# A pad of 1,344 bytes that gives all operands of two feed-forward layers one SBUF offset

## The chip, the cores and the metric

The kernel runs on one core of a Trainium2 chip. The metric is the device time of one execution in microseconds (us); the profile's span runs from the first to the last instruction of that execution.

## The reference, cut to what matters

Attention over 4 x 8 heads of 576 positions (a window of 32, half of the heads dilated by 4) gives 2,304 tokens of 512 features. Two feed-forward layers follow, 512 to 2,048 to 512, all in float32:

```python
x = attention(q, k, v)                       # (2304, 512)
h = x @ w_in                                 # 512 -> 2048
g = np.maximum(h, 0.0) + alpha * np.minimum(h, 0.0)
x = g @ w_out                                # 2048 -> 512
h = x @ w2_in
g = np.where(h >= 1, h, np.where(h <= -1, 0.0, (h + 1) ** 2 / 4))
return g @ w2_out
```

## The kernel before, in words

**The feed-forward work.** Each layer `ph` (0 or 1) goes through five tiles of tokens: four of 512 and one of 256 (the fourth in the first layer, the last in the second). A tile is written (ph, t) here. Within a tile, `f` runs over the 16 blocks of 128 hidden features. A pair (tile, f) is a slot; there are 160.

For each slot there are two groups of twelve matmuls: four blocks `c` of 128 features, by three products. `f_h` (lines 334 to 336, the **h group**) makes the block of h in one PSUM bank. `f_y` (lines 374 to 376, the **y group**) adds the block's part of the output to four PSUM banks. Float32 accuracy comes from three products: every operand is split into a rounded part (`xh`, `wih`, `gh`, `woh`) and the rest (`xl`, `wil`, `gl`, `wol`), and high x high, high x low and low x high are summed. Each matmul streams 512 (or 256) columns of x or g and has 128 x 128 weights of its own, loaded anew.

In iteration k the loop issues `f_h` of slot k, then `f_y` of slot k - 2. So h and y groups alternate, and h of block f is followed by y of block f - 2 (h(0) by y(14) of the tile before, h(1) by its y(15)). At the very end, y(13), y(14) and y(15) follow each other. In front of each y group and behind it, `attention_point` may put in a stage of attention: scores, transposed weights, values or output. There are 24 attention groups; six run before the loop, and the rest are spread over the first layer's first tiles.

Beside TensorE, ScalarE and VectorE make g from h (`f_g`, `f_cut`), ScalarE and GpSimd split the next block of output weights (`wo_split`, lines 320 and 321), and VectorE unpacks weights in the tiles that prepare a layer.

**Where the operands lie.** The SBUF pools are opened in the order const, wp, cv_p, xs_p, s_p, st_p (lines 75 to 80) and lie in memory in that order. Later, behind them, come sp, for the first attention groups, and then in its place wl_p, ws_p and g_p (lines 507, 509, 510). What the feed-forward matmuls read:

- `wih`, `wil`: for f < 8 in wp, for f >= 8 in wl_p
- `xh`, `xl`: in xs_p, four buffers each
- `woh`, `wol`: in ws_p, two buffers each (those of the last slot alone in cv_p)
- `gh`, `gl`: in g_p, two buffers each

All these tiles are 128 x 512 of 4 bytes, 2,048 bytes per partition, and all other tiles of wp, cv_p, xs_p, wl_p, ws_p and g_p are 2,048 or 4,096 bytes. So within a pool every tile starts at the same offset modulo 2 KB. Between xs_p and the late pools lie s_p (three tiles of 1,536 bytes) and st_p (two tiles of 24 bytes with three buffers each, in slots of 32 bytes).

Of the kernel before, what the change touches and what calls it, by code (L numbers as in the profile page):

```python
# [10 lines left out]
F32 = mybir.dt.float32  # L11
# [11 lines left out]
P = 128  # L23
# [24 lines left out]
)  # L48
TW = 512
WARM = 10  # L50
DS = D + 1

EARLY = (5, 6)
# [18 lines left out]
def attention_then_two_ffns(ctx: ExitStack, tc: tile.TileContext, a0, aqk, av, w1i, w1o, w2i, w2o, alpha, masks, ident, out):  # L72
# [8 lines left out]
    ps_h = ctx.enter_context(tc.tile_pool(name="ps_h", bufs=2, space=bass.MemoryType.PSUM))  # L81
    ps_a = ctx.enter_context(tc.tile_pool(name="ps_a", bufs=1, space=bass.MemoryType.PSUM))

    X = [const.tile([P, NT], F32, name=f"X{c}") for c in range(NC)]
    al = const.tile([P, NF], F32, name="al")
    mask = const.tile([P, NSB, KEYS], BF16, name="mask")
# [3 lines left out]
    qk = [const.tile([P, QK + KW], F32, name=f"qk{i}") for i in range(2)]  # L90
    vz = [const.tile([P, GS, 2, 4, DS], F32, name=f"vz{i}") for i in range(2)]

# [21 lines left out]
    def a_scores(i, pool, tag, add_on_pe):  # L114
# [20 lines left out]
        mx = st_p.tile([P, 2 * GS], F32, tag="mx", name="mx")  # L135
        nc.vector.tensor_reduce(mx, src, AX.X, ALU.max)
        sc_t[i] = (src, s, mx)
# [30 lines left out]
    def e_exp(i):  # L168
# [4 lines left out]
        mx = mx.rearrange("p (h n) -> p h n", h=2)  # L173
        nc.vector.tensor_reduce(mx, src, AX.X, ALU.max)
        nc.vector.tensor_tensor(
# [4 lines left out]
    def e_values(i):  # L180
# [3 lines left out]
        for n in range(GS):  # L184
            for j in range(4):
                r = slice(j * SUB, (j + 1) * SUB)
                for h in range(2):
                    p = slice(h * D, (h + 1) * D)
                    nc.tensor.matmul(ps[r, h, n * DS:(n + 1) * DS], pT[p, n, r], v[p, n, j], start=True, stop=True)  # L189
        a_norm(i, ps[:, :, :GS * DS].rearrange("p h (n d) -> p n h d", n=GS))  # L190

# [9 lines left out]
    def a_values(i, pool, tag):  # L201
        pT = pT_t.pop(i)
        ps = pool.tile([P, GS, 2, DS], F32, tag=tag, name="o_ps")
        for n in range(GS):
# [5 lines left out]
    def a_norm(i, ps):  # L210
        o = tmp(i).tile([P, GS, 2, D], F32, tag="o", name="o")
        rs = st_p.tile([P, GS, 2, 1], F32, tag="rs", name="rs")
        nc.vector.tensor_scalar(rs, ps[:, :, :, D:], 1e-9, None, ALU.add)
        nc.vector.reciprocal(rs, rs)
        nc.vector.tensor_tensor(o, ps[:, :, :, :D], rs.to_broadcast([P, GS, 2, D]), ALU.mult)
        o_t[i] = o

    def a_out(i, pool, tag):
# [8 lines left out]
        while at < len(subs):  # L227
# [4 lines left out]
            src = ps[:, at * SUB:(at + n) * SUB]  # L232
            xb = X[hp][:, b * S:(b + 1) * S]
            p0, p1 = s0 * SUB, (s0 + n) * SUB
# [66 lines left out]
    def x_split(n, c, on_pool=False):  # L301
# [3 lines left out]
        lo = xs_p.tile([P, TW], F32R, tag="xl", name="xl")  # L305
        src = X[c][:, t0:t0 + w]
        nc.scalar.activation(hi[:, :w], src, AF.Copy)
# [56 lines left out]
    def f_y(n, f):  # L364
# [12 lines left out]
        if f == NF - 1:  # L377
            for c in range(NC):
                dst = X[c][:, t0:t0 + w]
                if c % 2:  # L380
# [15 lines left out]
    with tc.manual_schedule(), ExitStack() as late:  # L396
        first = ExitStack()
        sp = first.enter_context(tc.tile_pool(name="sp", bufs=1))
        ps_e = first.enter_context(tc.tile_pool(name="ps_e", bufs=1, space=bass.MemoryType.PSUM))
        e_in = [sp.tile([P, QK + GS * 4 * DS], F32, name=f"e_in{i}") for i in range(NGB)]  # L400

# [28 lines left out]
        ps = ps_h.tile([P, TW], F32, tag="h", name="warm_ps")  # L430
        for _ in range(WARM):
            nc.tensor.matmul(ps, warm[:, :P], warm, start=True, stop=True)
# [170 lines left out]
def _attention_layout(q, k, v):  # L603
# [10 lines left out]
    ak = np.zeros((B, NGB, P, KW), q.dtype)  # L614
    av = np.ones((B, NSB, P, 4, DS), q.dtype)
    for sb in range(NSB):
# [53 lines left out]
```

## Time and profile before

| | |
|---|---|
| time, median of 3 runs | 891.58 us (890.82 to 891.71) |
| the profiled execution's own time | 891.61 us |
| its span | 889.8 us |
| TensorE busy | 871.0 us (98%), 5,470 matmuls |
| VectorE, ScalarE, GpSimd busy | 461.6, 371.6, 277.0 us |
| mean granted clock of TensorE | 0.987 |

How to read it: PE is TensorE's matmuls, PEld its weight loads, DVE VectorE, ACT ScalarE, POOL GpSimd. Matmuls are pipelined, so the durations of neighbours overlap: a row's duration is not the pace. The pace is the difference between the starts of rows that follow each other. In the timeline a line L334 that comes after a line L376 is the head of an h group, a line L374 after a line L336 the head of a y group; lines 334, 335, 336 then repeat for the four blocks c.

### The profile page before, as it was taken

To read this page: it belongs to the slowest core of one execution; us is meant where nothing else is said; L and a number is where in the kernel's file an instruction comes from. 1 tells how busy PE (TensorE), PEld (TensorE's weight loads), DVE (VectorE), ACT (ScalarE), POOL (GpSimd) and SP (SyncE) were. 2 spreads that over 40 slices of the span, in tenths; PEclk is the share of its full clock that TensorE was granted. 3 is DMA by queue.
4 is the path that set the end of the run, shared out by engine and by line. 5 is a ranking of instruction groups with operands and counts; after the bars stand their busy time and mean duration, and the time that the engine had idled before them with its cause. 6 is when DMAs were issued, how large, how long until landed. Compare 5 with 4: busy or idle time off the path is not lost.

```text
span 889.8 us, 13837 instructions
## 1 busy us (share of the span) xinstructions
PE 871.0 (98%) x5470; PEld 717.8 (81%) x5470; DVE 461.6 (52%) x769; ACT 371.6 (42%) x715; POOL 277.0 (31%) x222
## 2 busy tenths in 40 slices
PE   6889999999999999999999999999999999999998
PEld 3567778888888888998888888888888888888898
DVE  6788774433353423347776894543344334433443
ACT  3444445444354434454334343433343334333454
POOL 3355544121122122444442342222222222222243
PEclk8789999999999999999999999999999999999999
DMA  9696631131221400002442320010001000100100
GB/s 360 202 273 196 196 92 38 39 75 38 57 57 38 137 1 1 1 1 77 148 143 66 129 79 0 1 48 1 0 1 48 1 0 1 48 1 0 48 2 24
DMA packets 24832, 59.34 MB, mean 67 GB/s; under 512 B 2880, under 2 KB 10688, under 8 KB 24768
## 3 DMA queue, kind: packets, MB, share of 16 engines
q1 hardware_dynamic: 24480, 58.30, 21.0%
q8 instruction: 43, 0.70, 0.3%
q14 instruction: 21, 0.17, 0.1%
q10 hardware_dynamic: 288, 0.16, 0.1%
HBM read 53.73 MB, written 4.72 MB: 66 GB/s over the span
## 4 chain that ended last, share of the span: by engine, by line
PE 95%; DMA 2%; DVE 1%; ACT 1%; issue 1%; SPq 0%; ACTq 0%
PE h_ps L334 15%; PE y L374 15%; PE y L376 15%; PE h_ps L336 15%; PE y L375 15%; PE h_ps L335 15%; DMA e_in<-a 2%; PE s_ps L129 2%; PE o_ps L207 1%; PE x_ps L222 1%; PE t_ps L196 1%; DMA qk<-aqk 1%; PE o_ps L189 0%; PE s_ps L165 0%; ACT pT L198 0%
## 5 line engine op out<-in xcount | busy, mean ns | idle before, releaser
L321 POOL TENSOR_TENSOR wol<-wo,woh 128x512 fp32r<-128x512 f32 x160 | 207.8, 1299 | 481.6 <-ACT woh L320 481.6
L334 PE MATMUL h_ps<-xh,wil 128*128 128x512 f32 (+1 forms) x640 | 242.2, 378 | 0.4 <-DVE gl L362 0.3
L374 PE MATMUL y<-gh,wol 128*128 128x512 f32 (+1 forms) x640 | 239.3, 374 | 0.0
L336 PE MATMUL h_ps<-xh,wih 128*128 128x512 f32 (+1 forms) x640 | 237.9, 372 | 0.0
L376 PE MATMUL y<-gl,woh 128*128 128x512 f32 (+1 forms) x640 | 236.8, 370 | 0.0
L335 PE MATMUL h_ps<-xl,wih 128*128 128x512 f32 (+1 forms) x640 | 236.7, 370 | 0.0
L375 PE MATMUL y<-gh,woh 128*128 128x512 f32 (+1 forms) x640 | 236.0, 369 | 0.0
L334 PEld LDWEIGHTS h_ps<-xh,wil 128*128 128x128 f32 x640 | 121.2, 189 | 23.5 <-DVE gl L362 2.0
L336 PEld LDWEIGHTS h_ps<-xh,wih 128*128 128x128 f32 x640 | 120.9, 189 | 22.8
L374 PEld LDWEIGHTS y<-gh,wol 128*128 128x128 f32 x640 | 120.6, 188 | 21.7 <-issue 1.8
L376 PEld LDWEIGHTS y<-gl,woh 128*128 128x128 f32 x640 | 120.4, 188 | 21.8
L335 PEld LDWEIGHTS h_ps<-xl,wih 128*128 128x128 f32 x640 | 121.2, 189 | 20.7
L375 PEld LDWEIGHTS y<-gh,woh 128*128 128x128 f32 x640 | 120.6, 188 | 20.5
L353 ACT ACTIVATE g<-g,half 128x512 f32<-128x512 f32 (+1 forms) x80 | 54.5, 681 | 147.4 <-DVE g L352 147.2
L349 DVE SCALAR_TENSOR_TENSOR g<-g,al,h_ps 128x512 f32<-128x512 f32 (+1 forms) x80 | 55.3, 692 | 86.7 <-ACT g L347 86.5
L320 ACT ACTIVATE woh<-wo 128x512 fp32r<-128x512 f32 x160 | 99.2, 621 | 0.0
L356 ACT ACTIVATE gh<-g 128x512 fp32r<-128x512 f32 (+1 forms) x80 | 47.2, 589 | 120.5 <-PE y L375 80.1
L352 DVE TENSOR_SCALAR g<-h_ps 128x512 f32<-128x512 f32 (+1 forms) x80 | 50.8, 635 | 70.5 <-PE h_ps L336 70.3
L355 DVE TENSOR_TENSOR h_ps<-h_ps,g 128x512 f32<-128x512 f32 (+1 forms) x80 | 51.7, 646 | 58.9 <-ACT g L353 58.9
L362 DVE TENSOR_TENSOR gl<-h_ps,gh 128x512 fp32r<-128x512 f32 (+1 forms) x80 | 51.0, 637 | 56.6 <-ACT gh L356 56.6
L362 DVE TENSOR_TENSOR gl<-g,gh 128x512 fp32r<-128x512 f32 (+1 forms) x64 | 40.0, 626 | 70.7 <-ACT gh L356 62.8
L356 ACT ACTIVATE gh<-h_ps 128x512 fp32r<-128x512 f32 (+1 forms) x80 | 44.4, 555 | 71.4 <-PE y L375 48.2
(66 smaller groups left out, 581.2 us busy)
## 6 DMA issues: line engine op xcount, KB each, us to landing
st<-w1i SPq DMA_DIRECT2D x16, 512.0 KB, 5.0
st<-w1o SPq DMA_DIRECT2D x16, 512.0 KB, 4.5
st<-w2i SPq DMA_DIRECT2D x16, 512.0 KB, 3.4
st<-w2o SPq DMA_DIRECT2D x16, 512.0 KB, 3.3
qk<-aqk SPq DMA_DIRECT2D x36, 208.0 KB, 3.9
vz<-av SPq DMA_DIRECT2D x36, 195.0 KB, 3.9
out_t<-X SPq DMA_DIRECT2D x16, 256.0 KB, 2.0
e_in<-a SPq DMA_DIRECT2D x6, 416.0 KB, 7.4
```

The source lines that it names most:

```text
L320: nc.scalar.activation(hi, wf, AF.Copy)
L321: nc.gpsimd.tensor_tensor(lo, wf, hi.bitcast(F32), ALU.subtract)
L334: nc.tensor.matmul(ps[:, :w], wl[:, cs], xh[:, :w], start=(c == 0), stop=False)
L335: nc.tensor.matmul(ps[:, :w], wh[:, cs], xl[:, :w], start=False, stop=False)
L336: nc.tensor.matmul(ps[:, :w], wh[:, cs], xh[:, :w], start=False, stop=(c == NC - 1))
L349: nc.vector.scalar_tensor_tensor(t, t, al[:, f:f + 1], ps, ALU.mult, ALU.add)
L353: nc.scalar.activation(t, t, AF.Square, bias=half, scale=0.5)
L356: nc.scalar.activation(hi, ps, AF.Copy)
L362: (nc.gpsimd if n == order[0] else nc.vector).tensor_tensor(lo, ps, hi.bitcast(F32), ALU.subtract)
L374: nc.tensor.matmul(o, wl[:, cs], gh, start=(f == 0), stop=False)
L375: nc.tensor.matmul(o, wh[:, cs], gh, start=False, stop=False)
L376: nc.tensor.matmul(o, wh[:, cs], gl, start=False, stop=(f == NF - 1))
```

## The change

A pool of one tile of 336 float32 values (1,344 bytes per partition) that nothing reads or writes is opened after the last of the early pools and kept to the end. All that is allocated later, sp first and then wl_p, ws_p and g_p, moves up by 1,344 bytes. Nothing else is changed.

```diff
 WARM = 10
+
+PAD = 336
 DS = D + 1
...
     ps_h = ctx.enter_context(tc.tile_pool(name="ps_h", bufs=2, space=bass.MemoryType.PSUM))
     ps_a = ctx.enter_context(tc.tile_pool(name="ps_a", bufs=1, space=bass.MemoryType.PSUM))
 
+
+    ctx.enter_context(tc.tile_pool(name="pad", bufs=1)).tile([P, PAD], F32, name="pad")
     X = [const.tile([P, NT], F32, name=f"X{c}") for c in range(NC)]
```

## Rows read from the trace of the kernel before

**Rows 1.** The page: busy time by engine, and the chain that ended last.
```profile
PE 871.0 (98%) x5470; PEld 717.8 (81%) x5470; DVE 461.6 (52%) x769; ACT 371.6 (42%) x715; POOL 277.0 (31%) x222
...
PE 95%; DMA 2%; DVE 1%; ACT 1%; issue 1%; SPq 0%; ACTq 0%
```

**Rows 2.** Busy time by stretch: its ends, its length, engines, clock, DMA share, GB/s.
```profile
395.50:834.30 438.80, 438.73 (x1922) 358.80 (x1922) 237.88 (x355) 171.56 (x288) 124.27 (x96) 1.00 0.12 40
```

**Rows 3.** Groups by line and form: count | busy us, mean ns | idle before.
```profile
L334 PE MATMUL h_ps<-xh,wil 128*128 128x512 f32 x512 | 206.0, 402 | 0.1
```

**Rows 4.** Timeline of TensorE (start, duration): heads of h(0), h(8), next h(0), tile (1, 2).
```profile
657.84 0.39 PE L334 MATMUL h_ps<-xh,wil 128*128 128x512 f32 x1
...
701.79 0.40 PE L334 MATMUL h_ps<-xh,wil 128*128 128x512 f32 x1
...
746.05 0.39 PE L334 MATMUL h_ps<-xh,wil 128*128 128x512 f32 x1
```

**Rows 5.** Timeline, tile (1, 2): h(2), then y(0), its fourth matmul, then h(3).
```profile
668.83 0.39 PE L334 MATMUL h_ps<-xh,wil 128*128 128x512 f32 x1
...
671.59 0.39 PE L374 MATMUL y<-gh,wol 128*128 128x512 f32 x1
...
672.28 0.39 PE L374 MATMUL y<-gh,wol 128*128 128x512 f32 x1
...
674.32 0.39 PE L334 MATMUL h_ps<-xh,wil 128*128 128x512 f32 x1
```

**Rows 6.** The same: h(10), its fourth matmul, y(8), its fourth, then h(11).
```profile
712.86 0.40 PE L334 MATMUL h_ps<-xh,wil 128*128 128x512 f32 x1
...
713.56 0.39 PE L334 MATMUL h_ps<-xh,wil 128*128 128x512 f32 x1
...
715.62 0.40 PE L374 MATMUL y<-gh,wol 128*128 128x512 f32 x1
...
716.32 0.40 PE L374 MATMUL y<-gh,wol 128*128 128x512 f32 x1
...
718.39 0.40 PE L334 MATMUL h_ps<-xh,wil 128*128 128x512 f32 x1
```

**Rows 7.** Timeline, tile (0, 2): fourth matmul of h(3) after attention, then y(1).
```profile
267.85 0.39 PE L334 MATMUL h_ps<-xh,wil 128*128 128x512 f32 x1
...
269.89 0.39 PE L374 MATMUL y<-gh,wol 128*128 128x512 f32 x1
```

**Rows 8.** Timeline, the last tile's end: h(15), y(13), y(14) with its second, y(15).
```profile
880.29 0.28 PE L334 MATMUL h_ps<-xh,wil 128*128 128x256 f32 x1
...
881.71 0.29 PE L374 MATMUL y<-gh,wol 128*128 128x256 f32 x1
...
883.15 0.28 PE L374 MATMUL y<-gh,wol 128*128 128x256 f32 x1
883.27 0.28 PE L375 MATMUL y<-gh,woh 128*128 128x256 f32 x1
...
884.59 0.28 PE L374 MATMUL y<-gh,wol 128*128 128x256 f32 x1
```

**Rows 9.** Groups by line and form: the attention's scores.
```profile
L129 PE MATMUL s_ps<-qk 128*32 128x128 f32 x432 | 16.0, 284 | 0.7 <-DMA qk<-aqk 0.7
```

**Rows 10.** Timeline, the last tile: heads of h(4), y(2) and h(5).
```profile
848.89 0.28 PE L334 MATMUL h_ps<-xh,wil 128*128 128x256 f32 x1
...
850.32 0.28 PE L374 MATMUL y<-gh,wol 128*128 128x256 f32 x1
...
851.73 0.28 PE L334 MATMUL h_ps<-xh,wil 128*128 128x256 f32 x1
```

## The prediction

> **What bounds the kernel now.** I read the page's busy shares first. TensorE is busy 98% of the span and makes 95% of the chain that ended last; VectorE, ScalarE and GpSimd stand at 52%, 42% and 31% [rows 1]. In the stretch from 395.5 to 834.3 us, which holds the last 512-token tile of the first layer and four tiles of the second, TensorE is busy 438.73 of 438.80 us at a granted clock of 1.00, the 2.4 GHz level [rows 2]. It waits for nobody there, so the time is the number of matmuls times their pace, and nothing counts that does not change the pace.
>
> The pace is uneven. The busy means (402 ns for a 512-column matmul, [rows 3]) overlap and do not give it; starts in the timeline do. Tile (1, 2) is plain: its heads for f = 0, f = 8 and the next tile's f = 0 lie at 657.84, 701.79 and 746.05 us [rows 4]. Each half is eight iterations of an h and a y group, 192 equal matmuls, yet the halves take 43.95 and 44.26 us, 88.21 together.
>
> Inside one iteration of each half [rows 5, 6]:
> - f = 2: h takes 671.59 - 668.83 = 2.76 us, y 2.73 us; the last nine matmuls of that y take 674.32 - 672.28 = 2.04 us, 226.7 ns each.
> - f = 10: h takes 2.76 us, y 2.77 us; the last nine of y 2.07 us, the last nine of h 715.62 - 713.56 = 2.06 us, 229 ns each.
>
> **Operand offsets.** Every tile that these matmuls read is 2,048 bytes long, so its offset modulo 2 KB is that of its pool. wp and xs_p share one offset, call it A. Between them and the late pools lie s_p (3 x 1,536 bytes) and st_p (2 x 3 slots of 32), 4,800 bytes, or 704 past two times 2 KB. So wl_p, ws_p and g_p lie at B = A + 704. An h group with f < 8 reads weights and x at A; with f >= 8 it reads weights at B and x at A; a y group reads both at B (the last of all has its weights in cv_p, at A). A y group is the same in both halves: same buffers, same offsets, same PSUM banks. What differs is the h group that it follows. After one with both operands at A it takes 2.73 us, after one with weights at B 2.77 us. So a group carries the trace of the offset step in front of it.
>
> That trace dies out. In tile (0, 2) an h group at A and A comes after attention work, and its last nine matmuls run at 269.89 - 267.85 = 2.04 us, 226.7 ns each [rows 7], where h(2), just after a step from B to A, needs 2.76 us for twelve (230). The fast end of y, the fast end of this h and twelve times 226.7 (2.72 us) are my price for a group without a step. Where the offsets in a group differ (f >= 8) its end stays at 229.
>
> Nearest to a boundary without a step is the end of the kernel: y(13) and y(14) of the last tile follow each other, both at B. y(14) runs from 883.15 to 884.59 us, 1.44 us, at 0.12 a matmul from the first one on [rows 8]; nothing is disturbed at the boundary. That tile has 256 columns, so it shows the mechanism and not the price at 512.
>
> **The change, part by part.** The pad adds 1,344 bytes behind st_p, and 704 + 1,344 = 2,048: all late pools move to A. No instruction is added, nor a wait or a transfer. sp and its successors move together, so which early tile a late one overlaps, and hence what it waits for, stays. The attention's operands from X to st_p stay where they are. I cost all of that at nothing; were one of those waits longer, TensorE would show it as a gap.
>
> 1. Whole 512-column tiles without attention. 384 matmuls at 226.7 ns are 87.05 us against 88.21: 1.16 us per tile. There are five: -5.8 us.
> 2. Tiles (0, 0) to (0, 2) have 96 groups with attention matmuls between many of them: the 432 score matmuls recorded are 18 attention groups of 24 [rows 9], and three stages of each break some 54 boundaries. About 40 remain without a break. They save 1.16 us / 32 = 36 ns each: -1.4 us. At a broken boundary I take no change. Bounds: if every such group also came to 226.7, 54 x 36 ns or 1.9 us less; if each got the slower y (2.77 for 2.73), 54 x 0.04 or 2.2 us more. I take the middle, since the h of [rows 7] shows that a break can also leave the pace nearly flat.
> 3. The two 256-column tiles get worse. At one offset throughout, y(14) takes 1.44 us. Now h(15), at differing offsets, takes 881.71 - 880.29 = 1.42, h(4) 850.32 - 848.89 = 1.43 and y(2) 851.73 - 850.32 = 1.41 us [rows 8, 10]. Per tile, 8 x 0.02 + 8 x 0.01 + 8 x 0.03 = 0.48 us: +0.9 us for both.
> 4. Other engines: a faster TensorE asks for g and the split weights 1% sooner. GpSimd, the slowest per instruction, is busy 124 of 439 us in the steady stretch [rows 2]; its slack covers this. Uncovered, a lost half microsecond per iteration would eat the whole gain.
>
> Sum: -5.8 - 1.4 + 0.9 = -6.3 us. The profiled execution took 891.61 us (889.8 span and 1.8 around it), 0.03 above the median of 891.58, so it stands for the runs: 885.3 us.
>
> The Trainium skill speaks against any of this. "TensorE: Matmul & The Clock Gate", Step-by-step: what each phase is for, says that TensorE reads the streamed operand and the weights through two independent SBUF ports, and that loading the next weights takes nothing from the running matmul. By that rule offsets would not matter and the sum would be nil. Here equal y groups take 2.73 and 2.77 us by the address of weights that others used before them, which that rule does not give.
>
> **Rivals.**
> - No change. The pace comes from the alternation of groups itself (new PSUM bank, a new moving buffer, the return from column block 3 to 0), and offsets only shift its pattern: after the change some groups are quicker, some slower. For it: h groups take 2.76 us in both halves although one has equal offsets and the other not. Against it: the two kinds of y. Time 891.6.
> - Slower: all groups lock into the slow pattern. h with f < 8 already has the wanted state, both operands at A, and takes 2.76. If this is what one offset gives once a group begins afresh, each y that now takes 2.73 goes to 2.77: 8 per tile x 0.04 x 5 = 1.6 us, some 0.4 us in the earlier tiles, and the 256-column term of 0.9. Time 894.5. It decides at the first matmuls after a boundary: there h would still need over 230 ns. Against it: this h comes after a step from B to A, and the h of [rows 7], at the same offsets, settles at 226.7.
> - Half the gain. Each group keeps a short disturbance at its first three matmuls, as y in [rows 5] (0.69 us for three), because the weights' column block goes back there. All groups then take 2.73: per tile 16 x 0.03 + 8 x 0.04 = 0.8 us, five tiles 4.0, the earlier ones 1.0, less 0.9. Time 887.5.
> - More gain. The broken boundaries settle too (1.9 us), and the locked pace lies 1 ns lower than two-decimal starts tell (some 2,400 matmuls, 2.4 us). Time 881 to 883.
>
> **How the numbers follow.** Forecast 0.55, half the gain 0.16, more gain 0.09, no change 0.11, slower 0.09. About 0.2% (1.8 us) is what a measurement of this kernel can tell from no change. Faster by more than that: the first three, 0.80. Same 0.11. Slower 0.09. The forecast's own range is 883 to 888, from the bounds in 2 and 1 ns per matmul downward; the range is widened to 882.0 at the end of more gain and to 889.5 for a short disturbance with the upper bound of 2, which leaves out no change and slower, the two together 0.20.
>
> **What would show it.** In tile (1, 2) of the changed kernel both halves should take the same, near 43.5 us, and h and y alike 2.72 us. The pace should be flat across the boundary of h and y. The 256-column groups should all take 1.44 us, 0.48 us per tile more than now. TensorE should still be busy throughout. I am wrong if the halves still differ, if h(2) still takes 2.76 us, or if gaps on TensorE appear that name GpSimd or ScalarE.

## The result, and the profile after

The changed kernel takes 883.85 us (median of 5 runs, 883.60 to 885.64), the kernel before 891.71 in the same series (890.82 to 892.28). The ratio is 0.9916, 95% interval 0.9905 to 0.9927: faster by 0.84%. Forecast were 885.3 us and the range 882.0 to 889.5. The profiled execution took 883.60 us, its span is 881.8 us.

The page of the changed kernel, where [rows 1] stood before: TensorE is as large a share of the span busy as it was, and the same 5,470 matmuls keep it busy 7.6 us less.

```profile
PE 863.4 (98%) x5470; PEld 717.2 (81%) x5470; DVE 461.9 (52%) x769; ACT 371.5 (42%) x715; POOL 275.5 (31%) x222
```

Where the time went shows in the busy time by stretch, cut at the heads of the tiles. The columns are those of [rows 2]. First the kernel before (tiles (0, 0) to (0, 3); the next five, of 512 columns, in one; the last tile and the end):

```profile
31.15:145.49 114.34, 108.39 (x843) 83.85 (x841) 85.81 (x142) 50.05 (x98) 55.43 (x45) 0.96 0.56 162
145.49:247.67 102.18, 102.18 (x713) 82.97 (x709) 38.90 (x77) 46.55 (x109) 21.73 (x17) 1.00 0.24 58
247.67:347.14 99.47, 99.47 (x635) 80.70 (x634) 37.73 (x69) 41.81 (x93) 20.79 (x16) 1.00 0.16 48
347.14:395.45 48.31, 48.31 (x385) 47.32 (x384) 16.86 (x34) 23.82 (x53) 20.76 (x16) 1.00 0.00 1
395.45:834.27 438.82, 438.75 (x1923) 358.82 (x1921) 237.91 (x355) 171.60 (x288) 124.27 (x96) 1.00 0.12 40
834.27:889.80 55.53, 51.62 (x409) 50.22 (x407) 23.41 (x54) 25.70 (x54) 22.01 (x17) 1.00 0.08 29
```

The same stretches of the changed kernel:

```profile
30.48:144.19 113.71, 107.17 (x843) 82.53 (x841) 86.76 (x146) 50.38 (x99) 56.07 (x45) 0.97 0.58 165
144.19:245.56 101.37, 101.37 (x712) 82.94 (x709) 38.94 (x76) 46.48 (x109) 21.60 (x17) 1.00 0.24 58
245.56:344.15 98.59, 98.59 (x634) 80.65 (x633) 37.77 (x69) 41.88 (x93) 20.63 (x16) 1.00 0.16 48
344.15:392.82 48.67, 48.67 (x385) 47.69 (x384) 16.89 (x35) 23.87 (x53) 20.68 (x16) 1.00 0.00 1
392.82:825.97 433.15, 433.02 (x1922) 358.58 (x1921) 237.72 (x355) 171.58 (x288) 123.23 (x96) 1.00 0.12 41
825.97:881.80 55.83, 51.95 (x409) 50.56 (x407) 23.50 (x54) 25.77 (x54) 21.90 (x17) 1.00 0.08 29
```

The five 512-column tiles lose 5.67 us, the first three 0.63, 0.81 and 0.88; the 256-column tiles gain 0.36 and 0.30. The first h group starts 0.67 us earlier (30.48 for 31.15). In the runs below that start moves between 29.5 and 31.8 us without order, so I count it to no cause. Together 8.0 us.

The timeline of TensorE in tile (1, 2), as in [rows 4, 6]: the heads of h(0), of h(8) and of h(10) with its fourth matmul, of y(8) with its fourth, of h(11) and of the next tile.

```profile
651.89 0.39 PE L338 MATMUL h_ps<-xh,wil 128*128 128x512 f32 x1
...
695.41 0.39 PE L338 MATMUL h_ps<-xh,wil 128*128 128x512 f32 x1
...
706.29 0.39 PE L338 MATMUL h_ps<-xh,wil 128*128 128x512 f32 x1
...
706.97 0.39 PE L338 MATMUL h_ps<-xh,wil 128*128 128x512 f32 x1
...
709.01 0.39 PE L378 MATMUL y<-gh,wol 128*128 128x512 f32 x1
...
709.69 0.39 PE L378 MATMUL y<-gh,wol 128*128 128x512 f32 x1
...
711.73 0.39 PE L338 MATMUL h_ps<-xh,wil 128*128 128x512 f32 x1
...
738.93 0.39 PE L338 MATMUL h_ps<-xh,wil 128*128 128x512 f32 x1
```

Both halves take 43.52 us where they took 43.95 and 44.26. The h group takes 2.72 us and so does the y group; in both, the last nine take 2.04 us and the first three 0.68, which is the same pace. Across 8 iterations it is 43.52 / 192 = 226.7 ns. The last tile, in place of [rows 8, 10]: h(8), y(6) and h(9) start 1.44 us apart, 120 ns a matmul.

```profile
852.10 0.28 PE L338 MATMUL h_ps<-xh,wil 128*128 128x256 f32 x1
...
853.54 0.28 PE L378 MATMUL y<-gh,wol 128*128 128x256 f32 x1
...
854.98 0.28 PE L338 MATMUL h_ps<-xh,wil 128*128 128x256 f32 x1
```

### The profile page after: what moved, and what is told of

Same layout as the page of the kernel before. It is cut to its first block, busy times and chain, and to the rows that moved or that the text cites. A ratio compares the mean times of both kernels' runs of the same rounds, so it can differ in the third digit from the quotient of the medians.

```text
span 881.8 us, 13837 instructions
## 1 busy us (share of the span) xinstructions
PE 863.4 (98%) x5470; PEld 717.2 (81%) x5470; DVE 461.9 (52%) x769; ACT 371.5 (42%) x715; POOL 275.5 (31%) x222
## 4 chain that ended last, share of the span: by engine, by line
PE 94%; DVE 3%; DMA 1%; issue 1%; ACT 1%; SPq 0%; ACTq 0%; DVEq 0%
PE y L378 15%; PE h_ps L338 15%; PE y L380 15%; PE y L379 15%; PE h_ps L340 14%; PE h_ps L339 14%; PE s_ps L133 2%; PE o_ps L211 1%; PE t_ps L200 1%; PE x_ps L226 1%; DMA qk<-aqk 1%; DMA mask<-masks 1%; DVE wo L283 0%; PE s_ps L169 0%; PE o_ps L193 0%
## 5 line engine op out<-in xcount | busy, mean ns | idle before, releaser
L338 PE MATMUL h_ps<-xh,wil 128*128 128x512 f32 (+1 forms) x640 | 239.3, 374 | 0.4 <-DVE gl L366 0.3
```

The lines of the kernel that those rows point to most:

```text
L338: nc.tensor.matmul(ps[:, :w], wl[:, cs], xh[:, :w], start=(c == 0), stop=False)
```

## The experiments

All but the last are one execution each, compared with one execution of the kernel before on the same chip: 892.12 us for step512, step128, y_apart and x_apart, 890.85 for the four x_up kernels, 892.15 for step256 and the two sweeps. The last was run several times, and so was its kernel before. "Pace" is the time from the head of h(5) to that of h(13) of a tile, divided by its 192 matmuls.

### What counts as one offset

**step512.** Pad of 832 bytes: the late pools lie 512 bytes below A.

```diff
-PAD = 336
+PAD = 208
```

> The pad is 832 bytes in place of 1,344, so the late pools lie 512 bytes below A (modulo 2 KB) and not at A. Theory (a step of the offset between groups disturbs the pace, and steps of 512 bytes do not count, since the weights of the four blocks c of one group already lie 512 bytes apart and the pace is flat over them): as with the change, 883.9 us, 512-column groups of 2.72 us everywhere. Rival (the full offset modulo 2 KB counts): disturbed groups as before, h near 2.76 us, 889 to 892 us.

Measured: 883.27 us. The heads of h(0), h(8) and the next h(0) of tile (1, 2) lie 43.52 us apart, as with the change:

```profile
651.53 0.39 PE L338 MATMUL h_ps<-xh,wil 128*128 128x512 f32 x1
...
695.05 0.39 PE L338 MATMUL h_ps<-xh,wil 128*128 128x512 f32 x1
```

**step256.** Pad of 1,088 bytes: 256 below A. It was run after the x_up kernels further down, and its expectation rests on their paces (its 320 is x_apart's 1,344 modulo 512).

```diff
-PAD = 336
+PAD = 272
```

> The pad is 1,088 bytes, so the late pools lie 256 bytes below A. Theory (the unit is 256 bytes: distances of 64 and 320, of 128 and 384, of 0 and 256 gave alike paces): as with the change, all 512-column groups 2.72 us, 883 to 884.5 us. Rival (the unit is 512 bytes for steps): disturbed groups behind each boundary, 886 to 891 us.

Measured: 882.80 us, below the range expected, and the same 43.52 us:

```profile
651.09 0.39 PE L338 MATMUL h_ps<-xh,wil 128*128 128x512 f32 x1
...
694.61 0.39 PE L338 MATMUL h_ps<-xh,wil 128*128 128x512 f32 x1
```

**step128.** Pad of 1,216 bytes: 128 below A.

```diff
-PAD = 336
+PAD = 304
```

> The pad is 1,216 bytes, so the late pools lie 128 bytes below A. Theory: a step that is no multiple of 512 bytes disturbs the groups behind it, h with f < 8 and y above 2.72 us, h with f >= 8 settles at a pace other than 226.7 ns; 886 to 892 us. Rival (what counts is a smaller unit, 128 bytes or less): 883.9 us, all groups 2.72 us.

Measured: 889.78 us. Tile (1, 2): h(2), y(0), h(3); then h(10), y(8), h(11).

```profile
667.52 0.39 PE L338 MATMUL h_ps<-xh,wil 128*128 128x512 f32 x1
...
670.25 0.39 PE L378 MATMUL y<-gh,wol 128*128 128x512 f32 x1
...
672.98 0.39 PE L338 MATMUL h_ps<-xh,wil 128*128 128x512 f32 x1
...
711.33 0.40 PE L338 MATMUL h_ps<-xh,wil 128*128 128x512 f32 x1
...
714.12 0.39 PE L378 MATMUL y<-gh,wol 128*128 128x512 f32 x1
...
716.86 0.40 PE L338 MATMUL h_ps<-xh,wil 128*128 128x512 f32 x1
```

Here h and y with f < 8, where both operands step together, take 2.73 us: a step of 128 bytes disturbs them little (the first half of the tile takes 43.68 us for 43.52). But h(10), whose weights lie 128 bytes below x, takes 2.79 us, so most of this kernel's loss comes from the distance in such groups. By step512 and step256, what the change needs is one offset modulo 256 bytes, not 2 KB.

### Step or distance

Two kernels take the two halves of the explanation apart: steps without a distance, and a distance without steps.

**y_apart.** The change, and between wl_p and ws_p a second pad of 704 bytes.

```diff
         wl_p = late.enter_context(tc.tile_pool(name="wl_p", bufs=1))
         ps_y = late.enter_context(tc.tile_pool(name="ps_y", bufs=1, space=bass.MemoryType.PSUM))
+        late.enter_context(tc.tile_pool(name="pad_w", bufs=1)).tile([P, 176], F32, name="pad_w")
         ws_p = late.enter_context(tc.tile_pool(name="ws_p", bufs=2))
```

> The first pad stays, a second one of 704 bytes lies between wl_p and ws_p: all weights of h and x at A, all of y's operands at B. Every matmul has both operands at one offset, but each boundary of h and y is a step of 704 bytes. Theory (steps count): all iterations look like those with f < 8 of the kernel before, h 2.76 us, y 2.73 us, tile (1, 2) 87.9 us, 890 us in all. Rival (it is enough that the two operands of a matmul have one offset): 2.72 us everywhere, 884 us.

Measured: 888.96 us, tile (1, 2) 743.82 - 655.93 = 87.89 us. h(10), y(8), its fourth matmul, h(11):

```profile
710.86 0.39 PE L338 MATMUL h_ps<-xh,wil 128*128 128x512 f32 x1
...
713.62 0.39 PE L378 MATMUL y<-gh,wol 128*128 128x512 f32 x1
...
714.32 0.39 PE L378 MATMUL y<-gh,wol 128*128 128x512 f32 x1
...
716.36 0.39 PE L338 MATMUL h_ps<-xh,wil 128*128 128x512 f32 x1
```

2.76 us for h, 2.74 for y and 2.04 for its last nine: h(10) and y(8) now look like h(2) and y(0) in [rows 5], although each matmul has both operands at one offset. The step alone disturbs the groups, and its size counts: 704 bytes make it 43.95 us per half, where the 128 of step128 made 43.68 in the first half.

**x_apart.** No pad behind st_p, 1,344 bytes in front of xs_p and again in front of g_p.

```diff
+    ctx.enter_context(tc.tile_pool(name="pad_x", bufs=1)).tile([P, 336], F32, name="pad_x")
     xs_p = ctx.enter_context(tc.tile_pool(name="xs_p", bufs=4))
...
-    ctx.enter_context(tc.tile_pool(name="pad", bufs=1)).tile([P, PAD], F32, name="pad")
...
+        late.enter_context(tc.tile_pool(name="pad_g", bufs=1)).tile([P, 336], F32, name="pad_g")
         g_p = late.enter_context(tc.tile_pool(name="g_p", bufs=2))
```

> No pad behind st_p; 1,344 bytes in front of xs_p and 1,344 between ws_p and g_p: all weights at A, all streamed operands (x and g) 1,344 bytes above A modulo 2 KB, as x stands to the weights in h with f >= 8 before. No boundary has a step, but the operands of each matmul differ. Theory (steps disturb, a constant distance only sets another flat pace): flat from group to group at 229 ns for 512 columns and 118 ns for 256, tile (1, 2) 87.9 us in two equal halves, 256-column groups 1.42 us, 888 us in all. Rival (operands apart are disturbed all the time): uneven groups of 2.76 us and more, 891 us or above.

Measured: 889.43 us. Tile (1, 2): h(10), y(8), h(11); last tile: h(8), y(6), h(9).

```profile
711.67 0.39 PE L338 MATMUL h_ps<-xh,wil 128*128 128x512 f32 x1
...
714.41 0.39 PE L378 MATMUL y<-gh,wol 128*128 128x512 f32 x1
...
717.16 0.39 PE L338 MATMUL h_ps<-xh,wil 128*128 128x512 f32 x1
...
858.39 0.28 PE L338 MATMUL h_ps<-xh,wil 128*128 128x256 f32 x1
...
859.81 0.28 PE L378 MATMUL y<-gh,wol 128*128 128x256 f32 x1
...
861.22 0.28 PE L338 MATMUL h_ps<-xh,wil 128*128 128x256 f32 x1
```

The two 512-column groups together take 5.49 us, both halves of the tile 43.95 us, which is 228.9 ns a matmul; the 256-column groups take 1.41 to 1.42 us, 117.8 ns by the pace. Without a step the groups are alike; the distance sets the pace. Both parts of the explanation stand, and so does the time of [rows 6], 229 ns at the end of h(10).

### Is another distance better?

Four kernels with all weights at A and all streamed operands a constant distance d above (pads of 1,344 - d behind st_p, d in front of xs_p and d in front of g_p). For d = 64:

```diff
-PAD = 336
+PAD = 320
...
+    ctx.enter_context(tc.tile_pool(name="pad_x", bufs=1)).tile([P, 16], F32, name="pad_x")
     xs_p = ctx.enter_context(tc.tile_pool(name="xs_p", bufs=4))
...
+        late.enter_context(tc.tile_pool(name="pad_g", bufs=1)).tile([P, 16], F32, name="pad_g")
         g_p = late.enter_context(tc.tile_pool(name="g_p", bufs=2))
```

> All weights at A, all streamed operands 64 bytes above. No step at any boundary. Theory (without steps the groups are alike, and the constant distance between weights and streamed operand sets the pace): flat groups, at a pace of its own between the 224 and 234 ns seen so far, 882 to 893 us. Rival (only distance 0 gives 226.7 ns, every other one is slower): above 884 us. Rival (without steps the distance is of no account, as two independent read ports would have it): 883 to 884 us.

> The same with the streamed operands 256 bytes above the weights, half of 512. Theory: flat groups at a pace of its own, 882 to 893 us; if reading the same places at the same time is what costs, this distance is the best, and 512-column matmuls fall below 226.7 ns, the time below 883 us. Rival (only distance 0 is good): above 884 us. Rival (no account): 883 to 884 us.

> The same with 384 bytes. Theory: flat groups at a pace of its own, 882 to 893 us; near the 229 ns of 1,344 bytes (320 modulo 512) if neighbouring distances are alike. Rival (only distance 0 is good): above 884 us. Rival (no account): 883 to 884 us.

> The same with 448 bytes, 64 below the next multiple of 512. Theory: flat groups at a pace of its own, 882 to 893 us. Rival (only distance 0 is good): above 884 us. Rival (no account): 883 to 884 us.

Measured: 890.41, 884.75, 897.90 and 899.27 us. The groups were alike in each. With 448 bytes, h(5) and h(13) of tile (1, 2), then of the last tile:

```profile
692.32 0.40 PE L339 MATMUL h_ps<-xh,wil 128*128 128x512 f32 x1
...
737.12 0.40 PE L339 MATMUL h_ps<-xh,wil 128*128 128x512 f32 x1
...
860.84 0.28 PE L339 MATMUL h_ps<-xh,wil 128*128 128x256 f32 x1
...
882.60 0.28 PE L339 MATMUL h_ps<-xh,wil 128*128 128x256 f32 x1
```

That is 233.3 ns for 512 columns, the slowest of the four, and 113.3 for 256, the fastest. Half of 512 as the best distance was a miss: 256 bytes gave the 226.7 of 0. The 897.90 and 899.27 us lie above the 882 to 893 expected, and 384 bytes gave 232.3 ns, not a value near 229.

To see more distances in one run, two kernels make xh, xl, gh and gl 256 bytes longer and let each token tile put its data at an offset of its own (in floats):

```diff
+OFF = ([0, 3, 5, 44, 4], [8, 12, 24, 56, 52])
...
+        o = OFF[ph][t]
-        hi = xs_p.tile([P, TW], F32R, tag="xh", name="xh")
+        hi = xs_p.tile([P, TW + 64], F32R, tag="xh", name="xh")[:, o:o + w]
...
-        hi = g_p.tile([P, TW], F32R, tag="gh", name="gh")[:, :w]
+        hi = g_p.tile([P, TW + 64], F32R, tag="gh", name="gh")[:, o:o + w]
```

(xl and gl alike; the pad is 64 bytes, so that all late pools stay at A modulo 256.)

> xh, xl, gh and gl are 256 bytes longer and each token tile puts its data at its own distance above A in them: 0, 12, 20, 176 (256 columns), 16 bytes in the first layer, 32, 48, 96, 224, 208 (256 columns) in the second; weights stay at A. Theory (the distance modulo 256 sets the pace of a tile, and only a change of tile is a step): each tile flat behind its first groups, at a pace of its own; 512 columns near 226.7 to 229 ns for the distances up to 64, near 233 for 96, between 226.7 and 233.3 for 224; 256 columns between 113.3 and 119 ns for 176 and 208. About 886 us, more if the distances between those seen are worse. Rival (only multiples of 64 bytes matter): 12, 16, 20, 32 and 48 bytes all give 226.7.

> The same with 0, 80, 112, 240 (256 columns), 240 bytes in the first layer and 208, 160, 8, 4, 224 (256 columns) in the second. Theory: 8 and 4 bytes near 226.7 ns, 80, 112 and 160 between 229 and 234, 208 and 240 between 226.7 and 233.3; 256 columns between 113.3 and 120 ns for 224 and 240. About 888 us. Rival (only multiples of 64 bytes matter): steps of the pace at 64 and none between.

Measured: 899.15 and 896.70 us, where about 886 and 888 were expected. In sweep_b, h(5) and h(13) of tile (0, 4), distance 240, and of tile (1, 3), distance 4:

```profile
419.25 0.39 PE L340 MATMUL h_ps<-xh,wil 128*128 128x512 f32 x1
...
462.77 0.39 PE L340 MATMUL h_ps<-xh,wil 128*128 128x512 f32 x1
...
776.92 0.40 PE L340 MATMUL h_ps<-xh,wil 128*128 128x512 f32 x1
...
822.36 0.40 PE L340 MATMUL h_ps<-xh,wil 128*128 128x512 f32 x1
```

43.52 us against 45.44. The paces of the tiles without attention, from all of these runs (12, 20, 80 and 112 bytes lay in tiles with attention and are left out):

| distance, bytes modulo 256 | 512 columns, ns | 256 columns, ns |
|---|---|---|
| 0 (also 256) | 226.7 | 120.0 |
| 4 | 236.7 | |
| 8 | 233.3 | |
| 16 | 231.7 | |
| 32, 48, 96 | 233.3 | |
| 64 (also 1,344) | 228.9 | 117.8 |
| 128 (384) | 232.3 | 118.7 and 120.0 |
| 160 | 234.3 | |
| 176 | | 119.3 |
| 192 (448) | 233.3 | 113.3 (but see the last kernel) |
| 208 | 234.7 | 119.2 |
| 224 | 233.3 | 118.3 |
| 240 | 226.7 | 117.1 |

Both expectations were wrong about small distances: I thought 4 to 16 bytes near 226.7, as did the rival, and they cost 5 to 10 ns; 32 and 48 bytes cost 6.6. No distance tried beats 0 for 512 columns; 240 equals it. For 256 columns several are better than 0.

### A kernel that uses both

**both.** The change, with x and g 192 bytes further on inside their tiles in the two 256-column tiles only; they fill half of their buffers, so no space is needed.

```diff
+OFF = ([0, 0, 0, 48, 0], [0, 0, 0, 0, 48])
...
+        o = OFF[ph][t]
-        hi = xs_p.tile([P, TW], F32R, tag="xh", name="xh")
+        hi = xs_p.tile([P, TW], F32R, tag="xh", name="xh")[:, o:o + w]
...
-        hi = g_p.tile([P, TW], F32R, tag="gh", name="gh")[:, :w]
+        hi = g_p.tile([P, TW], F32R, tag="gh", name="gh")[:, o:o + w]
```

> The change as it is, and in the two 256-column tiles x and g lie 192 bytes further on within their tiles (the weights stay at A). Theory (the distance modulo 256 sets the pace): the 512-column groups stay at 2.72 us, the 256-column matmuls go from 120 to the 113.3 ns that 448 bytes (192 modulo 256) gave, 1.36 us for 1.44 per group; 64 groups x 0.08 = 5.1 us less, some 0.5 us given back at the steps between tiles: 879.3 us. Rival (448 bytes was good for another reason than its rest modulo 256, or the pace with 208 to 240 bytes, 117 to 119 ns, is what such a distance gives in these tiles): 882 to 883.5 us.

Measured: 881.36 us (median of 4, 880.83 to 882.41) against 890.56 for the kernel before (median of 7); ratio 0.9898, interval 0.9881 to 0.9914. That lies between the theory's 879.3 and the rival's 882. The interval overlaps that of the change (0.9905 to 0.9927), and the two were not timed in one series, so by the times alone it is not settled that this kernel is the faster one. The timeline shows what it gained: h(5) and h(13) of tile (0, 3); then, in the last tile, h(2), y(0), h(3), h(5) and h(13).

```profile
361.84 0.28 PE L340 MATMUL h_ps<-xh,wil 128*128 128x256 f32 x1
...
384.45 0.28 PE L340 MATMUL h_ps<-xh,wil 128*128 128x256 f32 x1
...
834.34 0.28 PE L340 MATMUL h_ps<-xh,wil 128*128 128x256 f32 x1
...
835.75 0.28 PE L380 MATMUL y<-gh,wol 128*128 128x256 f32 x1
...
837.62 0.39 PE L340 MATMUL h_ps<-xh,wil 128*128 128x256 f32 x1 [0.29 <-DVE gl L368]
...
843.25 0.28 PE L340 MATMUL h_ps<-xh,wil 128*128 128x256 f32 x1
...
865.01 0.28 PE L340 MATMUL h_ps<-xh,wil 128*128 128x256 f32 x1
```

Tile (0, 3) runs at (384.45 - 361.84) / 192 = 117.8 ns all through. The last tile begins so too (h(2) takes 1.41 us), TensorE then waits 0.29 us for VectorE's gl in front of h(3), and from h(5) on the pace is 113.3 ns (21.76 us for 192). One distance can have two steady paces, and what came before decides which one holds. In x_up384 the same pause (0.28 us) moved the last tile the other way, from 1.41 us a group to 1.44; in x_up448 tile (0, 3) ran at 113.3 without a pause. So a value of the table that one tile alone showed may be one of two. Against the profile of the change, tile (0, 3) is 0.83 us shorter (47.84 for 48.67) and the last stretch 2.00 (53.83 for 55.83), 2.8 us of the 5.1 expected; the slower pace in tile (0, 3) and at the start of the last one is what kept back most of the rest.

## Why the prediction was right

1. **The bound.** Right. In the stretch of the five tiles TensorE stays busy 433.02 of 433.15 us at a granted clock of 1.00; the gain there is pace.
2. **Whole 512-column tiles, -5.8 us.** Measured -5.67. The price of a group without a step, 2.72 us, was read from the undisturbed ends of groups in [rows 5, 7], and is what every unbroken group now takes. Some 0.1 us stays at the change from a 256-column tile to the next one and at single pauses.
3. **The first three tiles, -1.4 us.** Measured -2.32 (0.63, 0.81 and 0.88), the sum's largest miss. In the two timelines 46 groups of these tiles follow another feed-forward group directly and 46 follow attention; I had taken 40 and 54. From first to twelfth start the 46 unbroken ones save 1.61 us, 35 ns each, near the 36 I took. The 46 broken ones save 0.70 us, 15 ns each, where I took no change: that term, put at nothing, is most of the miss. Groups behind attention are still uneven after the change: in tile (0, 2), h(3) of [rows 7] starts at 264.82 and its fourth matmul at 265.59 us, 0.77 us where an unbroken group has 0.68. The value lies inside the bounds I gave (to -3.3). Tile (0, 0) also waits on loads and early attention, so its 0.63 us is not clean.
4. **The 256-column tiles, +0.9 us.** Measured +0.66 with the kernel's tail. Sign and pace (1.44 us per group) were right; not all groups had been at 1.41 to 1.43 before.
5. **Other engines at nothing.** Right: hardly a wait on TensorE in the steady stretch (0.13 us), and GpSimd's busy time there is 123.23 us against 124.27.
6. **The rivals.** No change and slower fell with the halves of 43.52 us. Half the gain fell with the first three matmuls of a group: 0.68 us, no disturbance where the weights' block goes back to c = 0. What the prediction drew from [rows 8], that a boundary without a step leaves no trace, holds at 512 columns too. More gain came in part: the broken boundaries gave the 0.70 us of item 3, but the pace was not below 226.7 ns. The upper end of the range is 889.7 by its own terms (887.5 and 2.2), not 889.5; nothing hangs on it.

At one granted clock, 1.00, the distance between weights and streamed operand moved the pace from 226.7 to 236.7 ns. The rule of independent read ports, from the Trainium skill's "TensorE: Matmul & The Clock Gate" (Step-by-step: what each phase is for), gives no such dependence, so here the measurement decides against what the prediction drew from it.

What the runs leave open is what makes the paces, and why one distance can have two. The unit of 256 bytes is shown by the pairs 0 and 256, 64 and 1,344, and by step256 and step512. Whether weight reads and stream reads hinder each other is shown by no run. The common offset A itself was not moved, and steps other than 128, 256, 512 and 704 bytes were not tried by themselves.

## What to carry to other kernels

When matmuls follow each other without a gap and still differ in pace, take differences of starts, not durations, and sort them by where their weights and streamed operands lie modulo 256 bytes. Put all operands of neighbouring matmuls at one remainder by a pad: here it cost 1,344 bytes per partition and bought 0.84%. The best distance depends on the number of columns, so measure a narrow tile by itself.

## What was unexpected

- 4 bytes between the remainders of weights and streamed operands cost 10 ns per 512-column matmul (236.7 against 226.7), more than any other distance tried; 240 bytes, 16 below the unit, cost nothing.
- 256 columns run at 120.0 ns with the distance that is best for 512, and at 113.3 with 192 bytes.
- One distance has two steady paces (117.8 and 113.3 ns in one execution), and a pause of TensorE can change one into the other; behind such a pause the 256-column matmuls became slower in x_up384 and faster in x_up448 and both.
- Without steps the pace is steady to the nanosecond: 43.52 us for each half of tile (1, 2), in three kernels with different pads.
